# Attention over channels with a gated convolution: v transposed by DMA in 16-bit halves instead of on TensorE

## The chip, the cores and the metric

The kernel runs on one core of one Trainium2 chip. The metric is device time in microseconds (us) of one execution. Its engines are TensorE (PE; PEld is its weight load), VectorE (DVE), ScalarE (ACT), GpSimd (POOL) and SyncE (SP), which issues most DMAs. Before the change it takes 657.74 us, the median of two runs (656.74 and 658.73).

## The reference

q, k and v have shape (4, 6336, 256) in fp32. Attention is over the 256 channels, not over the 6336 rows; its result goes through a causal convolution with a sigmoid gate.

```python
def _attn_ref(q, k, v, tau):
    qn = q / (np.linalg.norm(q, axis=1, keepdims=True) + 1e-06)
    kn = k / (np.linalg.norm(k, axis=1, keepdims=True) + 1e-06)
    s = kn.transpose(0, 2, 1) @ qn / tau
    s = s - s.max(-1, keepdims=True)
    a = np.exp(s)
    a /= a.sum(-1, keepdims=True) + 1e-09
    return v @ a
...
    for k in range(K):          # K = 5
        gate_pre += conv_w[k][None, None, :] * xp[:, k:k + S, :]
    gate = 1.0 / (1.0 + np.exp(-gate_pre))
    val = x @ w_val
    return gate * val @ w_out
```

Here x is the attention's result and xp is x with four rows of zeros ahead.

## The kernel before, in words

Two kinds of work run side by side, for four batches each.

**Scores** (`score_group`). The rows of q and k come in 17 groups of three blocks per batch. For each group ScalarE casts the block to a reduced fp32 form, `hi` (L192), GpSimd subtracts to get the rest (L193), ScalarE squares (L209), VectorE and GpSimd add up the squares for the norms (L214: `acc_ps` on VectorE, `acc` on GpSimd), and TensorE multiplies hi and lo halves into `s_ps` (L226). After 17 groups `softmax(b)` makes the weights of batch b, plain ones for the gate and ones multiplied with w_val for the value.

**Steps of v**. Each batch of v has 13 chunks, twelve of 508 rows and one of 240, in all 52 steps. With four rows of overlap a chunk is 512 columns wide once it is transposed. For each step:

- `load_v` (L310) loads the chunk, rows on partitions, by DMA from SP's queue (L317 to L323). For the first chunk of a batch GpSimd clears four rows (L316).
- `transpose_v` (L328) has TensorE turn it in blocks of 128x128 into `t_ps` (L335), once for each half of the channels. ScalarE casts the result to `v_hi` (L336) and VectorE subtracts to get `v_lo` (L337).
- `conv` multiplies with the weights into `x_ps` (L345); ScalarE takes the first tap (L359) and VectorE the other four (L361), for each half.
- `sigmoid` on ScalarE (L367), `value` on TensorE into `val_ps` (L345) with VectorE's product (L374), `split_g` with a cast on ScalarE (L387) and a subtraction on GpSimd (`g_lo`, L388).
- `finish` multiplies with w_out into `o_ps` (L404), ScalarE copies it out (L414) and its queue stores it (L419, L421).

Groups of the next batches run between the steps of the current one: the loop at L532 spreads the groups that are left over the first 36 steps, so the last steps have no scores beside them. `VLEAD = 2` has a chunk turned two steps ahead of its use; `v_p` holds three chunks of `v_hi` and `v_lo`. The order that a reader sees in the code is a wish: a scheduler places the instructions on each engine, and each engine, and each DMA queue, works through its own list in order. An instruction that waits holds up everything behind it on its engine.

Of the kernel before, what the change touches and what calls it, by code (L numbers as in the profile page):

```python
# [28 lines left out]
def kernel(  # L29
# [280 lines left out]
    def load_v(b, i):  # L310

        t0, w = chunks[i]
        t = raw_p.tile([P, NT, C], F32, name="v_raw", bufs=3)
        j0 = 0
        if i == 0:
            nc.gpsimd.memset(t[0:HALO, 0, :], 0.0)  # L316
            nc.sync.dma_start(out=t[HALO:P, 0, :], in_=v[b, 0:P - HALO])  # L317
            j0 = 1
        full, rest = divmod(HALO + w, P)
        lo = t0 - HALO  # L320
        nc.sync.dma_start(out=t[:, j0:full, :], in_=v[b, lo + j0 * P:lo + full * P].rearrange("(j p) c -> p j c", p=P))
        if rest:
            nc.sync.dma_start(out=t[0:rest, full, :], in_=v[b, lo + full * P:t0 + w])  # L323
        vraw[b, i] = t

    def transpose_v(b, i, h):
        w = HALO + chunks[i][1]
        if h == 0:  # L328
            vt[b, i] = [v_p.tile([P, NH, HALO + WMAX], F32R, name=name) for name in ("v_hi", "v_lo")]
        th, tl = vt[b, i]  # L330
        src = vraw[b, i]
        tp = ps.tile([P, 512], F32, name="t_ps", tag="bank")
        for j in range(-(-w // P)):
            np_ = min(P, w - j * P)
            nc.tensor.transpose(tp[:, j * P:j * P + np_], src[0:np_, j, h * P:(h + 1) * P], ident[0:np_, 0:np_])  # L335
        nc.scalar.copy(th[:, h, 0:w], tp[:, 0:w])  # L336
        nc.vector.tensor_tensor(tl[:, h, 0:w], tp[:, 0:w], th[:, h, 0:w].bitcast(F32), ALU.subtract)  # L337
# [269 lines left out]
```

## Time and profile before

| | |
|---|---|
| runs | 656.74 and 658.73 us, median 657.74 |
| profiled execution, first to last instruction (span) | 653.8 us |
| TensorE busy | 636.1 us, 97% |
| VectorE busy | 521.7 us, 80% |
| ScalarE busy | 465.7 us, 71% |
| GpSimd busy | 362.1 us, 55% |
| TensorE's granted clock | 0.999 of full |
| moved by DMA | 105.75 MB, mean 162 GB/s |

The profile is of one execution. The page gives no time of that execution beside its span; the runs' median is 3.9 us longer. A group row reads: line, engine, operation, out<-in with shapes, count, then busy time in us and mean ns of one, then the engine's idle time just before them and what ended it. Lines are those of the kernel before. Matmuls are pipelined, so that the durations of single ones overlap; the chain of waits shows what they take in sequence.

### The profile page before, as it was taken

To read this page: it belongs to the slowest core of one execution; us is meant where nothing else is said; L and a number is where in the kernel's file an instruction comes from. 1 tells how busy PE (TensorE), PEld (TensorE's weight loads), DVE (VectorE), ACT (ScalarE), POOL (GpSimd) and SP (SyncE) were. 2 spreads that over 40 slices of the span, in tenths; PEclk is the share of its full clock that TensorE was granted. 3 is DMA by queue.
4 is the path that set the end of the run, shared out by engine and by line. 5 is a ranking of instruction groups with operands and counts; after the bars stand their busy time and mean duration, and the time that the engine had idled before them with its cause. 6 is when DMAs were issued, how large, how long until landed. Compare 5 with 4: busy or idle time off the path is not lost.

```text
span 653.8 us, 10657 instructions
## 1 busy us (share of the span) xinstructions
PE 636.1 (97%) x4008; PEld 570.3 (87%) x4008; DVE 521.7 (80%) x831; ACT 465.7 (71%) x607; POOL 362.1 (55%) x174
## 2 busy tenths in 40 slices
PE   7999999999999999999998999999999999999996
PEld 5878799998979999999997998999999798988886
DVE  3897689787878688778788688778778889888894
ACT  5465978867888768668688787777777755655564
POOL 2441896965837769659565497766763122312221
PEclk9999999999999999999999999999999999999999
DMA  8999875555635665545554375653222343443213
GB/s 272 336 320 335 267 233 154 152 170 162 188 99 175 186 195 176 167 136 173 177 178 127 113 222 168 179 182 103 65 80 76 113 126 102 114 129 105 65 51 99
DMA packets 107875, 105.75 MB, mean 162 GB/s; under 512 B 5744, under 2 KB 107312, under 8 KB 107824
## 3 DMA queue, kind: packets, MB, share of 16 engines
q1 hardware_dynamic: 82048, 79.76, 39.8%
q10 hardware_dynamic: 25776, 25.32, 13.7%
q8 instruction: 31, 0.51, 0.3%
q14 instruction: 20, 0.16, 0.1%
HBM read 79.11 MB, written 25.95 MB: 161 GB/s over the span
## 4 chain that ended last, share of the span: by engine, by line
PE 84%; DVE 4%; ACT 4%; DMA 3%; SPq 2%; POOL 1%; issue 1%; ACTq 0%; DVEq 0%
PE o_ps L404 21%; PE x_ps L345 19%; PE val_ps L345 19%; PE s_ps L226 17%; PE t_ps L335 6%; SPq L74 2%; DMA raw<-in_k_dram 1%; PE o_ps L294 1%; POOL hi L193 1%; DMA w_raw<-in_moe_conv_w_dram 1%; DMA v_raw<-in_v_dram 1%; ACT hi L192 1%; DVE acc_ps L214 1%; DVE gate L361 1%; DVE gate L374 1%
## 5 line engine op out<-in xcount | busy, mean ns | idle before, releaser
L361 DVE SCALAR_TENSOR_TENSOR gate<-x_ps,wa,gate 128x508 f32<-128x508 f32 (+1 forms) x416 | 275.4, 718 | 14.4 <-ACT gate L359 13.4
L193 POOL TENSOR_TENSOR hi<-raw,hi 128x1536 fp32r<-128x1536 f32 (+2 forms) x54 | 167.8, 3109 | 92.8 <-ACT hi L192 92.8
L388 POOL TENSOR_TENSOR g_lo<-gate,g_hi 128x1016 fp32r<-128x1016 f32 (+1 forms) x50 | 116.8, 2335 | 145.1 <-ACT g_hi L387 130.5
L214 DVE TENSOR_TENSOR acc_ps<-acc_ps,sq 128x512 f32<-128x512 f32 (+1 forms) x134 | 93.5, 698 | 73.9 <-ACT sq L209 70.7
L345 PE MATMUL x_ps<-v_hi,w 128*128 128x512 f32 (+1 forms) x416 | 138.1, 391 | 0.0
L345 PE MATMUL val_ps<-v_hi,w 128*128 128x508 f32 (+1 forms) x416 | 133.9, 384 | 0.8 <-ACT o_sb L414 0.7
L226 PE MATMUL s_ps<-hi 128*128 128x256 f32 (+1 forms) x852 | 121.0, 287 | 6.2 <-ACT hi L192 4.0
L226 PEld LDWEIGHTS s_ps<-hi 128*128 128x128 f32 (+1 forms) x852 | 110.7, 190 | 12.6 <-ACT hi L192 5.5
L404 PE MATMUL o_ps<-wo_hi,g_hi 128*128 128x256 f32 x400 | 113.3, 283 | 0.2 <-DVE gate L374 0.2
L414 ACT COPY o_sb<-o_ps 128x512 f32<-128x512 f32 x99 | 58.1, 588 | 76.1 <-PE o_ps L404 74.8
L404 PE MATMUL o_ps<-wo_lo,g_hi 128*128 128x256 f32 x400 | 112.2, 281 | 0.0
L404 PE MATMUL o_ps<-wo_hi,g_lo 128*128 128x256 f32 x400 | 111.8, 280 | 0.0
L209 ACT ACTIVATE sq<-raw 128x1536 f32<-128x1536 f32 (+3 forms) x69 | 96.0, 1393 | 16.3 <-DVE acc_ps L214 8.0
L214 POOL TENSOR_TENSOR acc<-acc,sq 128x512 f32<-128x512 f32 x58 | 76.3, 1315 | 38.9 <-ACT sq L209 38.5
L345 PEld LDWEIGHTS val_ps<-v_hi,w 128*128 128x128 f32 x416 | 77.2, 188 | 14.4 <-ACT o_sb L414 0.9
L345 PEld LDWEIGHTS x_ps<-v_hi,w 128*128 128x128 f32 x416 | 77.5, 188 | 13.9 <-DVE gate L361 0.2
L359 ACT ACTIVATE gate<-x_ps,wa 128x508 f32<-128x508 f32 (+1 forms) x104 | 68.1, 669 | 20.6 <-PE x_ps L345 20.3
L336 ACT CAST v_hi<-t_ps 128x512 fp32r<-128x512 f32 (+1 forms) x104 | 55.7, 568 | 35.7 <-PE t_ps L335 33.2
L345 PE MATMUL x_ps<-v_lo,w 128*128 128x512 f32 (+1 forms) x208 | 79.8, 384 | 0.0
L345 PE MATMUL val_ps<-v_lo,w 128*128 128x508 f32 (+1 forms) x208 | 79.3, 381 | 0.0
L374 DVE TENSOR_TENSOR gate<-val_ps,gate 128x508 f32<-128x508 f32 (+1 forms) x104 | 64.3, 657 | 17.1 <-ACT gate L367 14.4
L404 PEld LDWEIGHTS o_ps<-wo_hi,g_hi 128*128 128x128 f32 x400 | 75.3, 188 | 1.4 <-DVE gate L374 0.4
(84 smaller groups left out, 800.0 us busy)
## 6 DMA issues: line engine op xcount, KB each, us to landing
raw<-in_q_dram SPq DMA_DIRECT2D x64, 384.0 KB
raw<-in_k_dram SPq DMA_DIRECT2D x64, 384.0 KB
v_raw<-in_v_dram SPq DMA_DIRECT2D x44, 512.0 KB
out_dram<-o_sb ACTq DMA_DIRECT2D x47, 384.0 KB
out_dram<-o_sb ACTq DMA_DIRECT2D x47, 124.0 KB
v_raw<-in_v_dram SPq DMA_DIRECT2D x4, 384.0 KB
raw<-in_q_dram SPq DMA_DIRECT2D x4, 128.0 KB
raw<-in_k_dram SPq DMA_DIRECT2D x4, 128.0 KB
```

The costliest lines, as they stand in the source:

```text
L193: nc.gpsimd.tensor_tensor(hi[r, js, :, 1, :], raw[r, js, :, :], hi[r, js, :, 0, :].bitcast(F32), ALU.subtract)
L209: nc.scalar.activation(sq[0:np_, ja:jb], raw[0:np_, ja:jb], AF.Square)
L214: eng.tensor_tensor(st[key][0:np_], st[key][0:np_], sq[0:np_, j], ALU.add)
L226: nc.tensor.matmul(st["s"][:, h, :], lhs, rhs, start=False, stop=stop and h == NH - 1 and n_ == len(ops) - 1)
L336: nc.scalar.copy(th[:, h, 0:w], tp[:, 0:w])
L345: marks["PRODUCT"] = nc.tensor.matmul(ps, wt[:, which, ws, ch, hs], vs[:, ch, lo:hi_], start=n_ == 0, stop=n_ == 3 * NH - 1)
L359: nc.scalar.activation(gate[:, h, 0:w], x_ps[:, 0:w], AF.Copy, scale=cw[:, h, 0:1])
L361: nc.vector.scalar_tensor_tensor(gate[:, h, 0:w], x_ps[:, tap:tap + w], cw[:, h, tap:tap + 1], gate[:, h, 0:w], ALU.mult, ALU.add)
L374: nc.vector.tensor_tensor(gate[:, h, 0:w], val_ps[:, 0:w], gate[:, h, 0:w], ALU.mult)
L388: nc.gpsimd.tensor_tensor(gl[:, :, 0:w], gate[:, :, 0:w], gh[:, :, 0:w].bitcast(F32), ALU.subtract)
L404: nc.tensor.matmul(o_ps[:, u * C:(u + 1) * C], gs[:, h, off:off + P], ws[:, h, :], start=n_ == 0, stop=n_ == 3 * NH - 1)
L414: marks["ACT"] = nc.scalar.copy(o_sb[:, j:j + len(pair), :], o_ps[:, 0:len(pair) * C].rearrange("p (j c) -> p j c", c=C))
```

## The change

v no longer goes through TensorE. Each 32-bit word of v is seen as two 16-bit halves, so a row of 256 channels is 512 half words. One DMA a chunk now loads v and transposes it in the same go (`dma_start_transpose`, `load_v`): half word number c lands on partition c mod 128, in one of four columns of 512 rows, `v_cols`. The two halves of a channel are then on neighbouring partitions. Four DMAs (`spread_v`, L330 in the new numbering) move them: each takes every second partition of two columns, 64 partitions with two runs of 1 KB, so that both halves of a channel come to lie on the channel's own partition in `v_parts`. VectorE interleaves them into whole words, `v_word`, with two copies of 16-bit elements that write every second half word (`join_v`, L345). ScalarE casts `v_word` to `v_hi` in one go (L346), and GpSimd, not VectorE, subtracts to get `v_lo` (L347). GpSimd's clearing of four rows is gone; VectorE clears four columns for the first chunk of a batch (L342). Loads start one step earlier than before. New pool: three buffers of `v_cols`, two of `v_parts`; `v_word` has two.

```diff
-    def transpose_v(b, i, h):
-        w = HALO + chunks[i][1]
...
-        for j in range(-(-w // P)):
-            np_ = min(P, w - j * P)
-            nc.tensor.transpose(tp[:, j * P:j * P + np_], src[0:np_, j, h * P:(h + 1) * P], ident[0:np_, 0:np_])
-        nc.scalar.copy(th[:, h, 0:w], tp[:, 0:w])
-        nc.vector.tensor_tensor(tl[:, h, 0:w], tp[:, 0:w], th[:, h, 0:w].bitcast(F32), ALU.subtract)
+    vx_p = ctx.enter_context(tc.tile_pool(name="vx_p", bufs=3))
...
+        t = vx_p.tile([P, 2 * NH, SPAN], U16, name="v_cols")
+        nc.sync.dma_start_transpose(out=t[:, :, 0:rows], in_=v[b, lo:lo + rows].bitcast(U16))
...
+    def spread_v(b, i):
+
+        t, rows = vcols.pop((b, i))
+        d = vx_p.tile([P, 2, NH, SPAN], U16, name="v_parts", bufs=2)
+        half = P // 2
+        for x in range(2):
+            for s in range(2):
+                nc.sync.dma_start(out=d[x * half:(x + 1) * half, s, :, 0:rows],
+                                  in_=t[s:P:2, x:2 * NH:2, 0:rows])
+        vparts[b, i] = d, rows
...
+        vw = v_p.tile([P, NH, HALO + WMAX], F32, name="v_word", bufs=2)
...
+        halves = vw.bitcast(U16).rearrange("p h (t s) -> p h s t", s=2)
+        for h in range(NH):
+            nc.vector.tensor_copy(halves[:, h, :, c0:c0 + n], d[:, :, h, rows - n:rows] if i else d[:, :, h, 0:n])
+        nc.scalar.copy(th[:, :, 0:HALO + w], vw[:, :, 0:HALO + w])
+        nc.gpsimd.tensor_tensor(tl[:, :, 0:HALO + w], vw[:, :, 0:HALO + w], th[:, :, 0:HALO + w].bitcast(F32), ALU.subtract)
...
+    load_v(*step(VLEAD + 1))
+    spread_v(*step(1))
+    join_v(*step(0))
...
-        if step(n + VLEAD + 1):
-            load_v(*step(n + VLEAD + 1))
+        if step(n + VLEAD + 2):
+            load_v(*step(n + VLEAD + 2))
...
         if new:
-            for h in range(NH):
-                transpose_v(*new, h)
+            join_v(*new)
+        if step(n + VLEAD + 1):
+            spread_v(*step(n + VLEAD + 1))
```

The change shifts the code's lines: what was L193, L214, L361, L374 and L388 is now L195, L216, L371, L384 and L398. Three places show how the lists of the engines change.

GpSimd, amid steps that run beside scores, before (`hi` is the split of q and k, `acc` the sum of squares, `g_lo` the split of the gated value):

```order
L388 TENSOR_TENSOR g_lo<-gate,g_hi 128x1016
L193 TENSOR_TENSOR hi<-raw,hi 128x6x256
L214 TENSOR_TENSOR acc<-acc,sq 128x512
L388 TENSOR_TENSOR g_lo<-gate,g_hi 128x1016
L193 TENSOR_TENSOR hi<-raw,hi 128x6x256
L214 TENSOR_TENSOR acc<-acc,sq 128x512
```

And with the change:

```order
L398 TENSOR_TENSOR g_lo<-gate,g_hi 128x1016
L347 TENSOR_TENSOR v_lo<-v_word,v_hi 128x1024
L398 TENSOR_TENSOR g_lo<-gate,g_hi 128x1016
L195 TENSOR_TENSOR hi<-raw,hi 128x6x256
L216 TENSOR_TENSOR acc<-acc,sq 128x512
L347 TENSOR_TENSOR v_lo<-v_word,v_hi 128x1024
L195 TENSOR_TENSOR hi<-raw,hi 128x6x256
L216 TENSOR_TENSOR acc<-acc,sq 128x512
```

One `v_lo` of 1024 columns a step has come in among the others.

VectorE in the same part of the program, before (`gate<-x_ps` are the taps, `gate<-val_ps` the product with the value):

```order
L374 TENSOR_TENSOR gate<-val_ps,gate 128x508 x2
L337 TENSOR_TENSOR v_lo<-t_ps,v_hi 128x512 x2
L361 SCALAR_TENSOR_TENSOR gate<-x_ps,wa,gate 128x508 x8
L214 TENSOR_TENSOR acc_ps<-acc_ps,sq 128x512 x2
L374 TENSOR_TENSOR gate<-val_ps,gate 128x508 x2
```

And with the change:

```order
L384 TENSOR_TENSOR gate<-val_ps,gate 128x508 x2
L371 SCALAR_TENSOR_TENSOR gate<-x_ps,wa,gate 128x508 x3
L345 COPY v_word<-v_parts 128x2x512 x2
L371 SCALAR_TENSOR_TENSOR gate<-x_ps,wa,gate 128x508 x5
L216 TENSOR_TENSOR acc_ps<-acc_ps,sq 128x512 x4
L384 TENSOR_TENSOR gate<-val_ps,gate 128x508 x2
```

Two copies stand in place of the two `v_lo`, here between the third and the fourth of eight taps.

SP's queue, which issues the loads, before:

```order
L74 DMA raw<-in_q_dram 128x3x256
L74 DMA raw<-in_k_dram 128x3x256
L321 DMA v_raw<-in_v_dram 128x4x256
L74 DMA raw<-in_q_dram 128x3x256
L74 DMA raw<-in_k_dram 128x3x256
```

And with the change:

```order
L76 DMA raw<-in_q_dram 128x3x256
L76 DMA raw<-in_k_dram 128x3x256
L330 DMA v_parts<-v_cols 64x2x512 x4
L76 DMA raw<-in_q_dram 128x3x256
L76 DMA raw<-in_k_dram 128x3x256
L320 DMA_TRANSPOSE v_cols<-in_v_dram 128x4x512
L330 DMA v_parts<-v_cols 64x2x512 x4
```

Beside the loads of q and k there are now five DMAs for a chunk of v where there was one, and the moves read what an earlier transposition wrote.

More of the change, by code (lines that the diff above doesn't have):

```diff
@@ L11 @@
 I32 = mybir.dt.int32
+U16 = mybir.dt.uint16
 I64 = mybir.dt.int64
@@ L306 @@
     NT = -(-(HALO + WMAX) // P)
-    vraw, vt = {}, {}
+    SPAN = NT * P
+    vcols, vparts, vt = {}, {}, {}
     def load_v(b, i):
         t0, w = chunks[i]
[L313 to L324, printed above, removed]
@@ L326, in transpose_v @@
-    def transpose_v(b, i, h):
-        w = HALO + chunks[i][1]
[L328 to L332, printed above, removed]
-        for j in range(-(-w // P)):
-            np_ = min(P, w - j * P)
-            nc.tensor.transpose(tp[:, j * P:j * P + np_], src[0:np_, j, h * P:(h + 1) * P], ident[0:np_, 0:np_])
-        nc.scalar.copy(th[:, h, 0:w], tp[:, 0:w])
-        nc.vector.tensor_tensor(tl[:, h, 0:w], tp[:, 0:w], th[:, h, 0:w].bitcast(F32), ALU.subtract)
+        lo = max(t0 - HALO, 0)
@@ new lines, in load_v @@
+        rows = -(-(t0 + w - lo) // 16) * 16
+        lo = min(lo, N - rows)
+        t = vx_p.tile([P, 2 * NH, SPAN], U16, name="v_cols")
+        nc.sync.dma_start_transpose(out=t[:, :, 0:rows], in_=v[b, lo:lo + rows].bitcast(U16))
+        vcols[b, i] = t, rows
+    def spread_v(b, i):
[7 more added lines that the diff above has]
+        vparts[b, i] = d, rows
@@ new lines, in join_v @@
+    def join_v(b, i):
+        t0, w = chunks[i]
+        d, rows = vparts.pop((b, i))
+        vw = v_p.tile([P, NH, HALO + WMAX], F32, name="v_word", bufs=2)
+        th, tl = vt[b, i] = [v_p.tile([P, NH, HALO + WMAX], F32R, name=name) for name in ("v_hi", "v_lo")]
+        n = w + (HALO if i else 0)
+        c0 = HALO + w - n
+        if c0:
+            nc.vector.memset(vw[:, :, 0:c0], 0.0)
+        halves = vw.bitcast(U16).rearrange("p h (t s) -> p h s t", s=2)
[3 more added lines that the diff above has]
+        nc.gpsimd.tensor_tensor(tl[:, :, 0:HALO + w], vw[:, :, 0:HALO + w], th[:, :, 0:HALO + w].bitcast(F32), ALU.subtract)
@@ L504 @@
         run_group()
-        for h in range(NH):
-            transpose_v(*step(0), h)
+    spread_v(*step(0))
     tick()
@@ L520 @@
         tick()
-    for h in range(NH):
-        transpose_v(*step(1), h)
+    spread_v(*step(2))
+    join_v(*step(1))
     with behind("ACT"):
@@ L567 @@
         if new:
-            for h in range(NH):
-                transpose_v(*new, h)
+            join_v(*new)
+        if step(n + VLEAD + 1):
+            spread_v(*step(n + VLEAD + 1))
         tick()
```

## The prediction

> **What bounds the kernel now.** I read the page's table of busy time first, then the chain that ended last, then the busy time of each engine in stretches.
>
> ```profile
> span 653.8 us, 10657 instructions
> PE 636.1 (97%) x4008; PEld 570.3 (87%) x4008; DVE 521.7 (80%) x831; ACT 465.7 (71%) x607; POOL 362.1 (55%) x174
> PE 84%; DVE 4%; ACT 4%; DMA 3%; SPq 2%; POOL 1%; issue 1%; ACTq 0%; DVEq 0%
> ```
>
> TensorE (PE) has work 97% of the time and 84% of the chain lies on it. GpSimd (POOL) shows 55%, but an average over stages hides where that work lies. These stretches show it (columns: PE, weight loads, DVE, ACT, POOL in us; last the clock, the DMA share and GB/s).
>
> ```profile
> 60.00:491.00 431.00, 426.21 (x2793) 386.37 (x2792) 345.03 (x550) 334.66 (x422) 300.23 (x133) 1.00 0.55 165
> 491.00:654.00 163.00, 155.54 (x982) 138.98 (x980) 133.04 (x218) 97.44 (x152) 40.90 (x20) 0.99 0.34 98
> ```
>
> In the first stretch each step of v shares the engines with scores of the next batch; I call it the score stage. There GpSimd is busy 300 of 431 us, VectorE (DVE) 345. The second stretch is the tail, with steps of v alone. TensorE's share of the transposes shows in the chain, in order of time, over one step of the tail (start, duration, what):
>
> ```profile
> 580.62 2.73 PE val_ps L345 x12
> 583.36 0.87 PE t_ps L335 x8
> 584.23 2.74 PE x_ps L345 x12
> 586.97 2.83 PE o_ps L404 x24
> 589.80 2.73 PE val_ps L345 x12
> ```
>
> The step takes 9.18 us, all of it TensorE, and 0.87 us are the eight transposes of one chunk of v. (Their row in the groups has 273 ns each, but they are pipelined; 0.87 us for eight is the price on the path.)
>
> **The change, part by part.** *Removed on TensorE:* 400 transposes, 50 times eight, 50 x 0.87 = 43.5 us; 37 chunks or 32 us of it in the score stage, 13 chunks or 11 us in the tail. If nothing else stood in the way that is the gain.
>
> *Moved to GpSimd:* the lo half. The rows of the groups by form:
>
> ```profile
> L337 DVE TENSOR_TENSOR v_lo<-t_ps,v_hi 128x512 fp32r<-128x512 f32 x96 | 63.1, 682 | 11.0 <-ACT v_hi L336 11.0
> L336 ACT CAST v_hi<-t_ps 128x512 fp32r<-128x512 f32 (+1 forms) x104 | 55.7, 568 | 35.7 <-PE t_ps L335 33.2 <-DMA out_dram<-o_sb 2.6
> L388 POOL TENSOR_TENSOR g_lo<-gate,g_hi 128x1016 fp32r<-128x1016 f32 x47 | 113.1, 2405 | 140.3 <-ACT g_hi L387 125.7 <-DMA raw<-in_k_dram 9.5 <-issue 5.2
> L193 POOL TENSOR_TENSOR hi<-raw,hi 128x1536 fp32r<-128x1536 f32 x44 | 154.8, 3519 | 86.6 <-ACT hi L192 86.6
> L316 POOL MEMSET v_raw<- 4x256 f32 x4 | 1.2, 303 | 0.0
> ```
>
> What costs DVE 2 x 0.68 us costs GpSimd one subtraction of 128x1024, which by g_lo's row takes 2.4 us. ScalarE's two casts (2 x 0.57 us) become one over the same elements, no price. Every step has one operation more on GpSimd (its order is shown with the change); in the whole order 37 v_lo stand ahead of the last hi, the split of q and k. So GpSimd's work in the score stage is 300.2 + 37 x 2.405 - 3 x 0.3 = 388 us, of the 431 us it has now. Queued behind a late v_lo are the next hi, which TensorE's score products wait for, and g_lo, which the output products wait for.
>
> *Added on VectorE:* two copies of 16-bit words a chunk, 1024 elements each, SBUF to SBUF. No row shows a 16-bit copy. The nearest are the weights' steps, 512 words of 32 bits SBUF to SBUF, seen in the timelines of DVE and of POOL (start, duration):
>
> ```profile
> 26.01 1.49 DVE L132 TENSOR_SCALAR wb<-w_raw 128x512 int32<-128x512 int32 x1
> ...
> 31.09 0.43 DVE L136 TENSOR_SCALAR wb<-w_raw 128x512 int32<-128x512 int32 x1
> ...
> 36.81 1.23 DVE L144 TENSOR_SCALAR w_raw<-w_raw 128x512 int32<-128x512 int32 x1
> ```
>
> ```profile
> 25.64 1.58 POOL L214 TENSOR_TENSOR acc<-acc,sq 128x512 f32<-128x512 f32 x1 [3.19 <-ACT sq L209]
> ...
> 36.47 1.28 POOL L214 TENSOR_TENSOR acc<-acc,sq 128x512 f32<-128x512 f32 x1 [3.21 <-ACT sq L209]
> ```
>
> Alone such a step takes 0.43 us; 512 elements out of PSUM take 0.68 (v_lo's row), so it moves about two elements a cycle. With 1024 elements a copy is then about 0.68 us, 1.36 a chunk, just what the two v_lo took; at one element a cycle it would be 1.2. I take 0.68, since the copy too goes from SBUF to SBUF with one input.
>
> The same rows show the real price. L132 takes 1.49 us where its like takes 0.43: a GpSimd operation ran from 25.64 to 27.22, and the step ended 0.28 us later. L144 took 1.23 us: GpSimd was busy until 37.75, and it ended 0.29 us after. Such a step waits until GpSimd's operation is over, and those last up to 3.5 us (hi's row). In the score stage GpSimd is nearly always busy, so the copies wait, and while one finishes GpSimd stands. For 512 elements that was 0.28 us; for 1024, with 0.27 us more, 0.55 us.
>
> [...]
>
> In VectorE's new order the copies stand amid the taps of the convolution: when they wait, the taps behind them wait, and with them the sigmoid and g_hi.
>
> *Added DMAs:* one transposition in place of the load, and four moves of 64 partitions, all on SP's queue. Prices of today:
>
> ```profile
> DMA packets 107875, 105.75 MB, mean 162 GB/s; under 512 B 5744, under 2 KB 107312, under 8 KB 107824
> q1 hardware_dynamic: 82048, 79.76, 39.8%
> q10 hardware_dynamic: 25776, 25.32, 13.7%
> v_raw<-in_v_dram SPq DMA_DIRECT2D x44, 512.0 KB
> ```
>
> The queues hold 54% of 16 engines for 653.8 us, or 353 us; a packet of about 1 KB costs 353 x 16 / 107875 = 52 ns, a chunk's 512 packets 1.7 us. The moves are again 512 runs of 1 KB: 1.7 us a chunk, hidden at 55% DMA. The transposition is in no trace. Below: the load's 1.7 us. Above: each row falls into four destination groups of 256 bytes, 2048 pieces; at a full packet's 52 ns each, 6.7 us a chunk. I take the low end, since bytes and engines stay the same, and keep the high end for a rival. Hidden either way in one chunk; what may be late is the q and k loads, which stand behind moves and transpositions in SP's new order. The moves wait for the copies that free their target, two chunks back, and the transposition for moves. At 431 / 37 = 11.6 us a step that is hidden, unless the copies are late.
>
> [...]
>
> *Start:* the first chunk's path grows by moves, copies and a longer lo half. Today it is (chain):
>
> ```profile
> 49.27 5.56 DMA v_raw<-in_v_dram
> 60.91 0.87 PE t_ps L335 x8
> 69.99 2.76 PE x_ps L345 x12
> ```
>
> Landing at 55, first use at 70. The moves stand behind three more pairs of loads on SP; with some 5 us for moves, 1.4 for copies, 1.0 for the cast and 2.4 for lo they use up the slack. I put 0 to 10 us, take 3.
>
> **The sum**, against the span of 653.8 us. Score stage: GpSimd 388 + 74 copies x 0.55 = 429 us, as long as the stage is now, without a single idle moment. Today it idles 131 of 431 us, by its rows waiting for ScalarE; some of that stays. I take 5%: 429 / 0.95 = 452, so +21 us (0%: -2; 10%: +46). TensorE's need, 426 - 32 = 394, lies below; what it saves hides behind GpSimd. VectorE: 345 plus waits of about a half operation (1.2 us) for half to all of the copies, 390 to 434: near the same end. Tail: -11 if TensorE alone decides; VectorE's step there is read from this stretch of five steps:
>
> ```profile
> 560.00:606.00 46.00, 46.00 (x284) 40.96 (x283) 39.40 (x61) 27.03 (x41) 12.03 (x5) 1.00 0.37 109
> ```
>
> 39.4 of 46 us, or 7.9 us a step. It stays 7.9, since the copies take what the v_lo took, and gets one or two waits of some 0.6 us (half a GpSimd operation, and GpSimd busy half the time: 4.8 us a step): 8.5 to 9.1, against 8.31 left for TensorE and 9.18 now. I take -5 for the tail. Start +3. In all 653.8 + 21 - 5 + 3 = 672.8. The runs' median, 657.74, lies 3.9 over the span, so **676.7 us**, 2.9% slower.
>
> **The rivals.** (a) *Faster:* the copies don't meet the wait, because a 16-bit step moves in another way than the 32-bit ones or GpSimd's gaps take them. Then GpSimd needs 388 / 0.95 = 409: -22; tail -8; start +3: 653.8 - 27 + 3.9 = 631. For: 131 us of gaps now. Against: five sixths and more of the stage would be filled.
> (b) *No change:* GpSimd runs with almost no idle time, its waits for ScalarE being only slack of a stage paced by TensorE: -2 - 5 + 3, so 654, up to 668 at 3% idle.
> (c) *Much slower, DMA decides:* each 256-byte piece costs a packet. Score stage: 0.55 x 431 = 237 us, plus 37 x (6.7 - 1.7 + 1.7) = 248, 485 of 431; at 95% full 510, +79; start +7: about 743. It decides from 5.2 us a transposition on (431 - 237 = 194 over 37), or 41 ns a piece. Against: the same bytes over the same engines.
> [...]
> That the transposes stay on TensorE is excluded: its order has none of v.
>
> **How the numbers follow.** The forecast's mechanism, with 3 to 10% idle, 0.44; a quarter of that stays within 2% (idle under 4%); (a) 0.20; (b) 0.18; (c) 0.18. About 2% (13 us) can be told from no change. Faster 0.20; same 0.18 + 0.11, about 0.30; slower 0.50. The likeliest case alone spans 668 to 702. The range reaches to (a) and well towards (c): 632 to 725.
>
> **What would show it.** Right: no t_ps; v_lo on POOL near 2.4 us; the copies' mean far above their least duration, long ones ending about 0.55 us after a POOL operation; POOL above 85% of the score stage; gaps of TensorE before score products that wait for hi. Steps in the tail between 8.3 and 9.2 us. Wrong: copies all near 0.68 us, or near 1.2; TensorE still without gaps (a); DMA share above 90% with VectorE waiting for v_parts (c).

## The result and the profile after

The changed kernel takes **727.0 us** (median of 724.4 and 729.7) against 657.74: a ratio of 1.106 (95% interval 1.095 to 1.116). The forecast was 676.7, range 632 to 725: the direction was right, but the time lies above the range, and the loss was 69 us and not 19. The profiled execution has a span of 722.6 us; by spans the loss is 68.8 us.

The page of the changed kernel, its head, DMA lines and the chain that ended last:

```profile
span 722.6 us, 10232 instructions
PE 629.2 (87%) x3608; PEld 550.4 (76%) x3608; DVE 608.2 (84%) x835; ACT 467.2 (65%) x557; POOL 498.4 (69%) x222
DMA packets 215491, 132.03 MB, mean 183 GB/s; under 512 B 112272, under 2 KB 214928, under 8 KB 215440
q1 hardware_dynamic: 189664, 106.06, 66.0%
PE 35%; DVE 25%; DMA 12%; issue 9%; POOL 7%; ACT 7%; SPq 3%; ACTq 0%; DVEq 0%; POOLq 0%
```

Before, 84% of the chain lay on TensorE; now 35%, with 25% on VectorE. TensorE has 400 instructions less and is busy nearly as long, which the sum of its time explains: before 636.1 busy + 17.7 idle; now 629.2 busy + 93.4 idle. Without the transposes (43.5 us on the path) it should be busy 592.6, and a kernel below that has nothing in their place is at 593.1. So of the 68.8 us, 75.7 are new idle time, 36.6 are matmuls that became slower, less the 43.5 saved. The groups, of the changed kernel, show both: where TensorE waits, and that its matmuls are longer (417 ns, 391 before).

```profile
L355 PE MATMUL x_ps<-v_hi,w 128*128 128x512 f32 (+1 forms) x416 | 152.0, 417 | 48.7 <-DVE gate L371 42.3
L345 DVE COPY v_word<-v_parts 128x1024 uint16<-128x1024 uint16 (+2 forms) x104 | 152.7, 1516 | 15.5 <-DMA v_parts<-v_cols 10.7
L347 POOL TENSOR_TENSOR v_lo<-v_word,v_hi 128x1024 fp32r<-128x1024 f32 (+1 forms) x52 | 122.6, 2357 | 33.3 <-ACT v_hi L346 30.8
L216 POOL TENSOR_TENSOR acc<-acc,sq 128x512 f32<-128x512 f32 x58 | 84.7, 1460 | 37.8 <-ACT sq L211 37.5
L228 PE MATMUL s_ps<-hi 128*128 128x256 f32 (+1 forms) x852 | 122.5, 294 | 8.3 <-POOL hi L195 6.3
```

The copies have a mean of 1516 ns; their quickest for 1024 words take about 0.7. TensorE waits 42.3 us for `gate` on VectorE, the taps that must read `x_ps` before its buffer is free. The order of events in one place, first VectorE, then GpSimd, then TensorE's waits, of which the first is from the start of the program (start, duration, what, idle before):

```profile
280.65 0.75 DVE L371 SCALAR_TENSOR_TENSOR gate<-x_ps,wa,gate 128x508 f32<-128x508 f32 x1
281.31 4.59 DVE L345 COPY v_word<-v_parts 128x1024 uint16<-128x1024 uint16 x2
285.81 0.72 DVE L371 SCALAR_TENSOR_TENSOR gate<-x_ps,wa,gate 128x508 f32<-128x508 f32 x1
```

```profile
280.07 3.54 POOL L195 TENSOR_TENSOR hi<-raw,hi 128x1536 fp32r<-128x1536 f32 x1
283.55 1.75 POOL L216 TENSOR_TENSOR acc<-acc,sq 128x512 f32<-128x512 f32 x1
285.27 3.94 POOL L195 TENSOR_TENSOR hi<-raw,hi 128x1536 fp32r<-128x1536 f32 x1
```

```profile
93.78 1.21 PE L355 MATMUL val_ps<-v_hi,w 128*128 128x508 f32 x2 [6.34 <-ACT v_hi L346]
...
286.58 0.49 PE L355 MATMUL x_ps<-v_hi,w 128*128 128x512 f32 x1 [2.61 <-DVE gate L371]
```

Two copies that need 1.4 us took 4.59. They end 0.6 us after GpSimd's operations end (283.6 and 285.3): each waited until the operation that was running was over, and the next operation of GpSimd is longer by about 0.4 (1.75 for 1.31, 3.94 for 3.54). This is the rule and not one case: of the 88 copies of 1024 words 43 take over 1 us, and each of these 43 ends 0.60 to 0.63 us after an operation of GpSimd. The tap behind them comes at 285.81, and TensorE, idle for 2.61 us, goes on after that tap.

The slow matmuls follow such gaps. Stretches of the changed kernel near its start (PE, weight loads, DVE, ACT, POOL; last the granted clock, DMA share, GB/s):

```profile
93.00:99.00 6.00, 5.22 (x22) 5.05 (x23) 6.00 (x7) 3.47 (x3) 5.58 (x3) 0.50 1.00 275
105.00:111.00 6.00, 5.82 (x19) 4.62 (x19) 5.41 (x10) 4.25 (x5) 2.50 (x2) 0.72 1.15 248
123.00:129.00 6.00, 6.00 (x36) 5.27 (x35) 5.38 (x10) 5.43 (x6) 5.43 (x2) 1.00 1.26 190
```

After 6.34 us idle (until 93.78) the granted clock is 0.50 for the next six, and TensorE is busy 5.22 us with 22 matmuls, 20 of them on 256 columns; at full clock 36 fit into 6 us, half of them on about 510 columns. The mean over the execution is 0.947, before 0.999; over the span that is (0.999 - 0.947) x 722.6 = 37.6 us, close to the 36.6 above. The rows show this much: a clock of 0.50 behind the gap (93 to 99), 0.72 from 105 to 111, and 1.00 in a stretch without one (123 to 129, TensorE busy 6.00 of 6.00). What length of gap brings the clock down, and how soon it is back, they don't show.

Where along the program the time goes is read from the start of the last product of q and k, the row of `s_ps`, of the kernel before and of the changed one:

```profile
L226 PE MATMUL s_ps<-hi x852: 275/283/468, 38.5 to 497.9; 128*128 128x256 f32 x169, 64*128 64x256 f32 x2
```

```profile
L228 PE MATMUL s_ps<-hi x852: 274/283/580, 37.4 to 565.2; 128*128 128x256 f32 x169, 64*128 64x256 f32 x2
```

Up to there 67.3 us are lost, after it 1.5 (155.9 and 157.4 us to the end). For places between I use the start of `g_lo`, one a step, as lag behind the kernel before: 15 us at step 1, 40 at step 7, 36 at step 13, 61 at 25, 70 at 37, 69 at 51. (Neighbouring steps can differ by up to 11 us near the start.) So about 36 us are gone after thirteen steps, 34 more by the end of the scores, and the tail wins nothing.

### The profile page after: what moved, and what is told of

Read it like the earlier page. It is cut to its first block, busy times and chain, and to the rows that moved or that the text cites. A ratio compares the mean times of both kernels' runs of the same rounds, so it can differ in the third digit from the quotient of the medians.

```text
span 722.6 us, 10232 instructions
## 1 busy us (share of the span) xinstructions
PE 629.2 (87%) x3608; PEld 550.4 (76%) x3608; DVE 608.2 (84%) x835; ACT 467.2 (65%) x557; POOL 498.4 (69%) x222
## 4 chain that ended last, share of the span: by engine, by line
PE 35%; DVE 25%; DMA 12%; issue 9%; POOL 7%; ACT 7%; SPq 3%; ACTq 0%; DVEq 0%; POOLq 0%
PE x_ps L355 11%; PE o_ps L414 10%; DVE v_word L345 9%; DVE gate L371 9%; PE val_ps L355 8%; PE s_ps L228 5%; DMA v_parts<-v_cols 5%; DMA out_dram<-o_sb 4%; DVE acc_ps L216 4%; POOL hi L195 3%; DMA raw<-in_k_dram 2%; POOL v_lo L347 2%; ACT sq L211 2%; ACT hi L194 2%; POOL acc L216 1%
## 5 line engine op out<-in xcount | busy, mean ns | idle before, releaser
L371 DVE SCALAR_TENSOR_TENSOR gate<-x_ps,wa,gate 128x508 f32<-128x508 f32 (+1 forms) x416 | 282.7, 718 | 32.1 <-ACT gate L369 29.1
L398 POOL TENSOR_TENSOR g_lo<-gate,g_hi 128x1016 fp32r<-128x1016 f32 (+1 forms) x50 | 119.8, 2396 | 113.9 <-ACT g_hi L397 109.5
L355 PE MATMUL x_ps<-v_hi,w 128*128 128x512 f32 (+1 forms) x416 | 152.0, 417 | 48.7 <-DVE gate L371 42.3
L195 POOL TENSOR_TENSOR hi<-raw,hi 128x1536 fp32r<-128x1536 f32 (+2 forms) x54 | 173.5, 3216 | 22.2 <-ACT hi L194 20.7
L345 DVE COPY v_word<-v_parts 128x1024 uint16<-128x1024 uint16 (+2 forms) x104 | 152.7, 1516 | 15.5 <-DMA v_parts<-v_cols 10.7
L347 POOL TENSOR_TENSOR v_lo<-v_word,v_hi 128x1024 fp32r<-128x1024 f32 (+1 forms) x52 | 122.6, 2357 | 33.3 <-ACT v_hi L346 30.8
L355 PEld LDWEIGHTS x_ps<-v_hi,w 128*128 128x128 f32 x416 | 83.4, 202 | 69.3 <-issue 32.7
L216 DVE TENSOR_TENSOR acc_ps<-acc_ps,sq 128x512 f32<-128x512 f32 (+1 forms) x134 | 92.9, 693 | 25.9 <-ACT sq L211 22.3
L216 POOL TENSOR_TENSOR acc<-acc,sq 128x512 f32<-128x512 f32 x58 | 84.7, 1460 | 37.8 <-ACT sq L211 37.5
L369 ACT ACTIVATE gate<-x_ps,wa 128x508 f32<-128x508 f32 (+1 forms) x104 | 67.7, 666 | 42.3 <-PE x_ps L355 32.8
L377 ACT ACTIVATE gate<-gate 128x1016 f32<-128x1016 f32 (+1 forms) x52 | 52.9, 1018 | 58.2 <-DVE gate L371 57.6
L355 PE MATMUL x_ps<-v_lo,w 128*128 128x512 f32 (+1 forms) x208 | 85.4, 411 | 0.2 <-POOL v_lo L347 0.2
L384 DVE TENSOR_TENSOR gate<-val_ps,gate 128x508 f32<-128x508 f32 (+1 forms) x104 | 64.1, 656 | 23.3 <-ACT gate L377 21.0
L346 ACT CAST v_hi<-v_word 128x1024 fp32r<-128x1024 f32 (+1 forms) x52 | 52.7, 1013 | 47.9 <-PE val_ps L355 27.2
```

What stands on the lines that cost most here:

```text
L195: nc.gpsimd.tensor_tensor(hi[r, js, :, 1, :], raw[r, js, :, :], hi[r, js, :, 0, :].bitcast(F32), ALU.subtract)
L216: eng.tensor_tensor(st[key][0:np_], st[key][0:np_], sq[0:np_, j], ALU.add)
L345: nc.vector.tensor_copy(halves[:, h, :, c0:c0 + n], d[:, :, h, rows - n:rows] if i else d[:, :, h, 0:n])
L347: nc.gpsimd.tensor_tensor(tl[:, :, 0:HALO + w], vw[:, :, 0:HALO + w], th[:, :, 0:HALO + w].bitcast(F32), ALU.subtract)
L355: marks["PRODUCT"] = nc.tensor.matmul(ps, wt[:, which, ws, ch, hs], vs[:, ch, lo:hi_], start=n_ == 0, stop=n_ == 3 * NH - 1)
L369: nc.scalar.activation(gate[:, h, 0:w], x_ps[:, 0:w], AF.Copy, scale=cw[:, h, 0:1])
```

## The experiments

Theories. **P**: VectorE's copies wait for GpSimd's operations, and the taps behind them, and TensorE behind those, are late; GpSimd's added `v_lo` makes the waits more. **O**: it is enough that copies stand in an engine's order amid the operations that TensorE waits for. **A** and **C**: the DMAs (the moves, the transposition) are late. **G**: GpSimd's added work alone bounds the score stage. The first four expectations were written under other names, which they explain.

Every run is compared with the kernel before, timed beside it (657.1 to 658.2 us).

| run | us | ratio (95% interval) |
|---|---|---|
| e1_plain_load | 729.9 | 1.109 (1.105 to 1.112) |
| e2_act_copies | 727.7 | 1.107 (1.103 to 1.111) |
| e3_no_vlo | 702.3 | 1.067 (1.064 to 1.071) |
| e4_before_plus_transposes | 693.0 | 1.054 (1.050 to 1.057) |
| e5_no_moves | 710.6 | 1.082 (1.078 to 1.087) |
| e6_no_v_dma | 706.7 | 1.076 (1.072 to 1.079) |
| e7_start_on_pe | 717.1 | no interval; four executions of 705.1 to 721.3 us |
| e8_tail_dma | 681.6 | 1.036 (1.034 to 1.039) |
| e9_act_copies_dve_lo | 737.6 | 1.124 (1.121 to 1.127) |
| e10_no_dma_no_lo | 661.3 | 1.006 (1.003 to 1.008), without one execution of 1277 us |
| e11_no_dma_no_copies | 624.8 | 0.951 (0.950 to 0.953) |
| e12_no_dma_no_copies_no_lo | 617.8 | 0.941 (0.939 to 0.942) |
| e13_tail_dve_copies | 670.3 | 1.021 (1.016 to 1.026) |
| e14_tail_pool_copies | 669.5 | 1.019 (1.016 to 1.022) |
| e15_no_dma_act_copies | 681.1 | 1.036 (1.033 to 1.040) |
| e16_no_dma_idle_pool | 653.0 | 0.993 (0.991 to 0.995) |
| e17_idle_pool_no_copies | 632.5 | 0.962 (0.959 to 0.965) |
| e18_one_copy | 707.7 | 1.073 (1.066 to 1.081) |

### First: one suspect at a time

**e1_plain_load**, the transposition replaced by a plain load of the same bytes:

```diff
-        nc.sync.dma_start_transpose(out=t[:, :, 0:rows], in_=v[b, lo:lo + rows].bitcast(U16))
+        nc.sync.dma_start(out=t[:, :, 0:rows], in_=v[b, lo:lo + rows].bitcast(U16).rearrange("(p j) c -> p (j c)", p=P).rearrange("p (a r) -> p a r", r=rows))
...
-            nc.vector.tensor_copy(halves[:, h, :, c0:c0 + n], d[:, :, h, rows - n:rows] if i else d[:, :, h, 0:n])
+            nc.vector.tensor_scalar(halves[:, h, :, c0:c0 + n], d[:, :, h, rows - n:rows] if i else d[:, :, h, 0:n], 0xBFFF, None, ALU.bitwise_and)
```

> The transposing load is a plain load of the same bytes in 4 KB runs; moves, copies, cast and the lo half stay (the values are then not v transposed, and the copy masks one bit so that all words are finite). Theory 1, the loss lies in VectorE's copies waiting for GpSimd and in GpSimd's added work: 710 to 727 us, the copies' mean stays near 1.5 us. Theory 2, the transposition's own price on the DMA engines sets it: the DMA share of the first 150 us falls from over 1.0 to about 0.85, the 35 to 40 us that were lost by the seventh step go, 680 to 692 us. If both hold: 685 us with the copies' mean still above 1.3 us.

729.9 us, no gain. Nor is the start any better: the lag is 12 us at step 1, 41 at step 7, 45 at step 13. What the transposition costs more than a load is not what was lost.

**e2_act_copies**, the two copies on ScalarE:

```diff
-            nc.vector.tensor_copy(halves[:, h, :, c0:c0 + n], d[:, :, h, rows - n:rows] if i else d[:, :, h, 0:n])
+            nc.scalar.copy(halves[:, h, :, c0:c0 + n], d[:, :, h, rows - n:rows] if i else d[:, :, h, 0:n])
```

> The two interleaving copies go to ScalarE, all else stays. Theory 1: no VectorE instruction of a step needs what GpSimd holds, so the 82 us of waiting in the copies go and the 36 us that were lost between steps 13 and 34 with them: 680 to 695 us; ScalarE gets about 104 us more work and ends near 85 per cent. Theory 2: the start stays as it is, 715 to 730 us, with a DMA share of over 1.0 in the first 150 us. If both hold: about 690 us, with the first seven steps still 30 us late.

```profile
PE 628.5 (87%) x3608; PEld 550.3 (76%) x3608; DVE 468.8 (65%) x731; ACT 579.3 (80%) x660; POOL 477.2 (66%) x222
```

727.7 us, though VectorE's busy time falls from 608 to 469. ScalarE is at 80% and TensorE now waits for its `g_hi` (17.9 us) and for GpSimd's `hi` (17.1). By itself this speaks against P; e15 takes it up.

**e3_no_vlo**, `v_lo` left out, the products read zeros:

```diff
-        th, tl = vt[b, i] = [v_p.tile([P, NH, HALO + WMAX], F32R, name=name) for name in ("v_hi", "v_lo")]
+        th = v_p.tile([P, NH, HALO + WMAX], F32R, name="v_hi")
+        vt[b, i] = th, vzero
...
-        nc.gpsimd.tensor_tensor(tl[:, :, 0:HALO + w], vw[:, :, 0:HALO + w], th[:, :, 0:HALO + w].bitcast(F32), ALU.subtract)
```

> The lo half of v is left out: the products use a tile of zeros in its place, so GpSimd has 122 us less work; copies stay on VectorE. Theory 1: GpSimd is busy as before the change, the copies wait about half as long (mean about 1.1 us), 690 to 705 us. Theory 2: 715 to 727 us, the start unchanged.

702.3 us, 25 less. At step 13 it has lost as much as the changed kernel (36 us), at step 51 49 and not 69: `v_lo` costs in the score stage, not at the start.

**e4_before_plus_transposes**, the kernel before with a transposition of each chunk that nobody reads:

```diff
         vraw[b, i] = t
+        x = vx_p.tile([P, 2 * NH, NT * P], U16, name="v_cols")
+        nc.sync.dma_start_transpose(out=x[:, :, 0:rows], in_=v[b, lo:lo + rows].bitcast(U16))
```

> The kernel before with the transposing load added beside its own load of v, its result unused; no moves, no copies, TensorE transposes as before. The bytes through DMA are those of the changed kernel. Theory 1: the transposition is hidden, 657 to 665 us. Theory 2: the DMA engines are full in the first 150 us and q and k come late: 675 to 695 us.

693.0 us. The loss comes in the first 16 steps (37 us at step 16) and stays there (36 at step 51). The engines' work is that of the kernel before, so these 35 us come from the queues, where each chunk is now fetched twice. It made me look for the lost time in the DMAs, and that was the wrong place.

### Second: the DMAs taken out

**e5_no_moves** and **e6_no_v_dma**:

```diff
-        d = vx_p.tile([P, 2, NH, SPAN], U16, name="v_parts", bufs=2)
...
+        d = t.rearrange("p (s h) r -> p s h r", s=2)
```

In e5 `v_cols` has five buffers, as many as `v_cols` and `v_parts` had together. e6 leaves out the moves too, and here is what it leaves out besides:

```diff
-        t = vx_p.tile([P, 2 * NH, SPAN], U16, name="v_cols")
-        nc.sync.dma_start_transpose(out=t[:, :, 0:rows], in_=v[b, lo:lo + rows].bitcast(U16))
+        t = vfix
```

> The four moves of a chunk are left out: the copies read the transposed columns where they landed (with the same sizes and strides), the bytes that become v are not v's, and the copy is an AND with 0xBFFF so that every word stays finite. Every chunk keeps its transposition, its two copies on VectorE, its cast and its lo half on GpSimd. The changed kernel has lost 40 us at g_lo of step 7 and 69 us at the end. Theory A (the start is late because the moves stand behind pairs of raw loads on SP and land late, and because transposition, moves and copies wait for each other in turn): the lag at step 7 falls under 15 us and the time to about 700 us. Theory B (the lost time comes from the copies and the lo half on the engines, DMA is hidden): lag and time stay, 720 to 730 us. Theory C (the transposition's long issue on SP holds up the raw loads): the lag at step 7 stays above 20, since the transposition is still there; 705 to 725 us.

> No byte of v is loaded, transposed or moved: the copies of every chunk read one constant tile of zeros that is set once at the start, so the results are not v's. The engines' work is that of the changed kernel (two copies on VectorE with an AND, one cast, one lo half on GpSimd a chunk, no transposes on TensorE); the DMA engines have less than in the kernel before. Theory A or C (what is lost at the start is DMA): the lag of g_lo at step 7 is under 10 us, and what remains is the engines' loss: the kernel before plus about 25 us for the lo half (what leaving it out gave) minus some us in the tail, 670 to 690 us. Theory B (the engines alone lose it): lag 35 to 45 us at step 7 and 715 to 730 us.

710.6 and 706.7 us: the moves are worth 16 us, the transposition 4, and 49 of 69 us are lost with no DMA of v at all. Lags of `g_lo`:

| step | changed | e5, no moves | e6, no DMA | e11, no copies |
|---|---|---|---|---|
| 1 | 15 | 14 | 3 | 0 |
| 7 | 40 | 30 | 12 | -1 |
| 13 | 36 | 24 | 19 | -5 |
| 37 | 70 | 63 | 54 | -26 |
| 51 | 69 | 61 | 52 | -30 |

At step 13 36 us are lost: 12 by the moves, 5 by the transposition, 19 by the engines, and after it the DMAs add nothing. From step 13 to 37 the three kernels lose the same, 34, 39 and 35 us. A and C are right on a quarter of the loss, the engines on the rest. The page and the groups of e6:

```profile
PE 623.8 (88%) x3608; PEld 548.4 (78%) x3608; DVE 611.9 (87%) x836; ACT 468.6 (66%) x557; POOL 499.1 (71%) x222
L351 PE MATMUL x_ps<-v_hi,w 128*128 128x512 f32 (+1 forms) x416 | 147.1, 407 | 37.2 <-DVE gate L367 33.3
L341 DVE TENSOR_SCALAR v_word<-vfix 128x1024 uint16<-128x1024 uint16 (+2 forms) x104 | 155.0, 1539 | 4.0 <-POOL v_lo L343 3.9
```

The copies are as long as with DMAs, 1539 ns, and TensorE waits for the same taps.

**e7_start_on_pe**, chunks 0 to 7 on TensorE, from 8 on by DMA:

```diff
+    def by_dma(b, i):
+        n = b * NC + i
+        return n >= 8
...
     def join_v(b, i):
+        if not by_dma(b, i):
+            for h in range(NH):
+                transpose_v(b, i, h)
+            return
```

> The first eight chunks are loaded row by row and transposed on TensorE as in the kernel before, with their lo halves on VectorE; chunks 8 to 51 go the changed way. The computation is complete. Theory A or C (a start-up loss, by chunks that are needed before their DMAs can be there): lag of g_lo at step 7 at most 8 us, no new loss of 35 us when the changed way begins at step 8, and 727 - 30 to 40 = 685 to 697 us. Theory D (each change to the DMA way costs the same lead wherever it begins, because VectorE's waits and the queue lose it in the first steps after the change): the lag is small at step 7 and reaches 30 us within eight steps after step 8; 715 to 727 us.

717 us in the median, 705 in the fastest of four: not the 685 to 697 of A or C, but about the 715 to 727 of theory D, by which the way of DMA loses the same wherever it begins. The trace is of an execution of 718 us. The lag is 0 at step 4, 11 at 8, 17 at 13, 31 at 17 and 60 at 37: half of the start's loss is saved (17 us at step 13 for 36), and from there to step 37 another 44 us are lost (34 to 39 in the three kernels with copies of the table). A loss at the start of the program is not the main part.

### Third: copies and lo half, one without the other

All without DMAs of v. **e10** leaves `v_lo` out of e6 (as e3 does), **e11** the copies (the diff, against e6), **e12** both:

```diff
-        vw = v_p.tile([P, NH, HALO + WMAX], F32, name="v_word", bufs=2)
+        vw = vfix.rearrange("p a r -> p (a r)").bitcast(F32).rearrange("p (h r) -> p h r", h=NH)
...
-        for h in range(NH):
-            nc.vector.tensor_scalar(halves[:, h, :, c0:c0 + n], d[:, :, h, rows - n:rows] if i else d[:, :, h, 0:n], 0xBFFF, None, ALU.bitwise_and)
```

> As the run without any DMA of v (constant zeros as source, 706.7 us), and the lo half is left out too (the products read a tile of zeros in its place); two copies on VectorE and one cast a chunk remain, and GpSimd has no more than the kernel before. Theory P: the copies still wait behind GpSimd at 55%, mean about 1.2 us; leaving the lo half out gave 25 us in the run with DMAs: 675 to 690 us. Rival (with the DMAs gone the lo half is all that is left): 650 to 660 us.

> As the run without any DMA of v, and the two copies are left out too (the cast and the lo half read a constant tile of words); the lo half stays on GpSimd, so GpSimd's work is that of the changed kernel, 500 us, and VectorE's is 522 - 63 = 459. [...] Theory P (the waits of the copies, which hold up the taps behind them, are most of it): 640 to 660 us. Theory G (GpSimd's added 2.4 us a chunk itself is the bound of the score stage): 680 to 700 us, with TensorE waiting for hi of GpSimd.

> No DMA of v, no copies, no lo half: of the work on v only the cast of a constant tile is left, and TensorE has no transposes. This is what the removal of the transposes would bring with all that replaces them free: 658 - 43.5 = 614 us if TensorE alone sets it, and about 625 to 640 if ScalarE, VectorE and GpSimd already set part of the steps in the kernel before.

| | no lo half | lo half on GpSimd |
|---|---|---|
| no copies | 617.8 (e12) | 624.8 (e11) |
| two copies on VectorE | 661.3 (e10) | 706.7 (e6) |

The lo half alone costs 7 us, the copies alone 43.5, both 89: 38 us arise only from the two together. G is out. A stretch of the score stage of e11:

```profile
60.00:460.00 400.00, 392.03 (x2482) 354.00 (x2481) 305.70 (x473) 326.94 (x380) 370.45 (x163) 1.00 0.42 127
```

GpSimd works 370 of 400 us, 93%, and TensorE 392 at full clock: a GpSimd that is nearly full delays nobody as long as VectorE has no copy to wait for it.

### Fourth: is it the wait, or the place in the order?

**e16** leaves GpSimd without work (the lo halves of q, k, v and g and its sums of squares), with the copies of e6; **e17** is e16 without copies. **e15** is e6 with ScalarE's copies, edited as in e2. Of e16 the lines for q and k:

```diff
-            nc.gpsimd.tensor_tensor(hi[r, js, :, 1, :], raw[r, js, :, :], hi[r, js, :, 0, :].bitcast(F32), ALU.subtract)
...
-            eng, key = (nc.vector, "acc") if j < nv else (nc.gpsimd, "side")
+            if j >= nv:
+                continue
+            eng, key = nc.vector, "acc"
```

> No DMA of v, the copies on VectorE as in the changed kernel, and GpSimd left without work: the lo halves of q, k, v and g and GpSimd's sums of squares are left out, and the products read zeros in their place, so that TensorE, VectorE and ScalarE have the same instructions as in the run without DMA and without v's lo half (661.3 us). Theory P: every copy takes about 0.7 us, VectorE's busy time falls from 587 to about 535 us, and the time falls to 618 to 630 us, that of the runs without copies. Theory O: the copies cost their 43 us still, 650 us or more, less what TensorE no longer waits for GpSimd (6 to 12 us).

> As the run with GpSimd left empty (653.0 us, every copy 0.74 us), with the copies left out too: the cast reads a constant tile of words. Theory O (a copy costs TensorE its place amid the taps in VectorE's order, without any wait for GpSimd): about 615 us, that is 35 to 40 us below. Theory P (only the waits for GpSimd cost, and the other order that the program takes when GpSimd is empty accounts for the rest): 640 to 650 us.

> As the run without any DMA of v (706.7 us, zeros as source), but with the copies on ScalarE, so that VectorE has no operation that can wait for GpSimd: VectorE 469 us, ScalarE 580, GpSimd 500. Theory P (the waits for GpSimd are what the copies cost): near the run without copies, 624.8, and ScalarE's 80% a little over it: 630 to 650 us. Theory O (it is the copies' place in an engine's order, amid operations for which TensorE waits): 690 to 710 us, as on VectorE.

The copies' durations in e16 (least, median, most in ns), and in e10, where GpSimd has the work of the kernel before:

```profile
L345 DVE TENSOR_SCALAR v_word<-vfix x104: 431/744/768, 3.7 to 594.5; 128x1024 uint16<-128x1024 uint16 x88, 128x1016 uint16<-128x1016 uint16 x8, 128x488 uint16<-128x488 uint16 x8
```

```profile
L344 DVE TENSOR_SCALAR v_word<-vfix x104: 433/759/4147, 3.7 to 612.3; 128x1024 uint16<-128x1024 uint16 x88, 128x1016 uint16<-128x1016 uint16 x8, 128x488 uint16<-128x488 uint16 x8
```

With GpSimd empty no copy takes over 0.77 us: the waits are for GpSimd, as P has it. But e16 was not down at 618 to 630: the copies cost 653.0 - 632.5 = 20.5 us without any wait. So O seems to have its part: 1.4 us a step on VectorE, in order, ahead of taps. How large it is stays unsure. e17 has less to do than e12 and takes 632.5 - 617.8 = 14.7 us longer; nothing is added in it, but the scheduler chose another order of instructions, so order alone may be worth that much between two of these kernels. With GpSimd's old work the copies cost 43.5 us, with `v_lo` too 706.7 - 624.8 = 81.9. If the 20.5 may be carried over, a quarter of that 82 is place and three quarters are waits; the 82, the 43.5 and the 38 of the table are well above what order did, the 20.5 is not. On ScalarE no copy takes over 1437 ns (mean 1319), so none waits once begun, and they cost 681.1 - 624.8 = 56 us: less than on VectorE, more than nothing. They are 129.6 us in all, on an engine that is then at 85%. Both theories were too simple, P as well as O.

**e18_one_copy**, the changed kernel with one copy of 2048 words for two of 1024:

```diff
-        for h in range(NH):
-            nc.vector.tensor_copy(halves[:, h, :, c0:c0 + n], d[:, :, h, rows - n:rows] if i else d[:, :, h, 0:n])
+        part = d[:, :, :, rows - n:rows] if i else d[:, :, :, 0:n]
+        nc.vector.tensor_copy(halves[:, :, :, c0:c0 + n], part.rearrange("p s h t -> p h s t"))
```

> The computation is complete: the changed kernel, with one copy of 2048 words a chunk in place of two of 1024. If a copy waits once for a GpSimd operation whatever its size, 52 waits of about 0.8 us are gone from VectorE: its busy time falls from 608 to about 570 us, and the time to 705 to 715 us. Rival (the second copy of a pair mostly follows the first without a new wait, or a copy with one more dimension is slower): 720 to 735 us and VectorE at 600 us or more.

```profile
PE 625.5 (88%) x3608; PEld 550.3 (78%) x3608; DVE 573.4 (81%) x783; ACT 464.7 (66%) x555; POOL 501.0 (71%) x222
L345 DVE COPY v_word<-v_parts 128x2048 uint16<-128x2048 uint16 (+2 forms) x52 | 114.9, 2209 | 22.0 <-DMA v_parts<-v_cols 13.8
```

707.7 us, VectorE 573: as P said. The same words in half as many instructions save 38 us of copy time (152.7 to 114.9) and 19 us in all. A copy's mean is 0.80 us above its median of 1.41 now (2.21), and was 0.75 above a median of 0.76 (1.52): a wait is paid per instruction. It need not be a wait for one operation only: the longest copy of e18 takes 10.3 us and ends after the fourth operation of GpSimd that ran meanwhile.

### Fifth: versions that might beat both

**e9_act_copies_dve_lo**, copies on ScalarE and `v_lo` on VectorE:

```diff
-        nc.gpsimd.tensor_tensor(tl[:, :, 0:HALO + w], vw[:, :, 0:HALO + w], th[:, :, 0:HALO + w].bitcast(F32), ALU.subtract)
+        nc.vector.tensor_tensor(tl[:, :, 0:HALO + w], vw[:, :, 0:HALO + w], th[:, :, 0:HALO + w].bitcast(F32), ALU.subtract)
```

> The computation is complete: DMAs as in the changed kernel, the two copies of a chunk on ScalarE and the lo half on VectorE, so GpSimd does no more than in the kernel before and no copy on VectorE can wait for it. By the busy times of the runs so far: GpSimd 362 us, VectorE 469 + 52 x about 1.1 = 526, ScalarE 579. Theory P (VectorE's copies waiting behind GpSimd's operations, and GpSimd's added work, are what TensorE waits for; the DMAs add about 20 us): 665 to 685 us. Theory O (every chain of small operations in order costs it, whichever engine has them; ScalarE at 80% passes its lateness on as VectorE did): 700 to 725 us, with TensorE waiting for ScalarE's g_hi and o_sb.

```profile
L347 DVE TENSOR_TENSOR v_lo<-v_word,v_hi x52: 656/1620/4508, 76.5 to 703.1; 128x1024 fp32r<-128x1024 f32 x48, 128x488 fp32r<-128x488 f32 x4
```

737.6 us, worse than all. I had counted on 1.1 us for this subtraction and on no wait. For 1024 columns it takes 1.21 us at least and up to 4.5, and each of the longest 25 ends 1.08 or 1.09 us after an operation of GpSimd: here both inputs are in SBUF, and it waits for GpSimd as the copies do. In the kernel before one input was in PSUM, and there the 96 subtractions of 512 columns all take 0.68 to 0.69 us. ScalarE's copies in turn waited 43.8 us for this `v_lo` to free their buffer.

**e8**, **e13**, **e14**: only the 13 chunks of the tail by DMA, with the copies on ScalarE, VectorE, GpSimd (`by_dma` as in e7, the diff against e7):

```diff
-        return n >= 8
+        return n >= B * NC - NC
```

> Chunks 0 to 38 are transposed on TensorE as in the kernel before; only the 13 chunks of the last batch, used when the score work is over and GpSimd, ScalarE and the DMA queues have room, go the changed way, with their two copies on ScalarE. The computation is complete. If TensorE alone sets a step of the tail (0.87 us of transposes in 9.18): 13 x 0.87 = 11 us less than the kernel before, 647 us, down to 645. Rival (in the changed kernel the tail won only about 3 us, so that something else soon ends each step, VectorE or the waits between engines): 654 to 660 us, no difference that can be told.

> The computation is complete. As the run that had only the 13 chunks of the last batch by DMA, but with their copies on VectorE as in the changed kernel instead of on ScalarE. In the changed kernel the last 13 steps won 3 to 5 us over the kernel before. If that holds when only they are changed, and the loss of the run with ScalarE's copies (+24 us) came from ScalarE's order: 652 to 657 us. Rival (the DMA way costs its 20 to 25 us at each place where it begins, by its first chunks): 675 to 685 us.

> The computation is complete. Only the last 13 chunks by DMA, their copies on GpSimd, which also has their lo half: GpSimd is busy 41 of 163 us in the tail of the kernel before, VectorE then has 1.36 us a step less and no operation that waits for GpSimd. If TensorE sets the step then: 8.31 for 9.18 us, 647 us. Rival (GpSimd's four operations a step, 2.4 + 2.4 and two copies of 1 to 2.4 us, fill its step, 7 to 9.6 us, and the lo half of g comes late): 655 to 670 us.

681.6, 670.3 and 669.5 us, all slower than before. In e13 the lag is 3 us up to step 35, 20 at step 43 and 14 at 51: the first chunks of the new way come late, as rows of VectorE show, and the last eight steps win 6 us.

```profile
501.88 1.37 DVE L387 COPY v_word<-v_parts 128x1016 uint16<-128x1016 uint16 x2 [2.46 <-DMA v_parts<-v_cols]
513.27 1.36 DVE L387 COPY v_word<-v_parts 128x1024 uint16<-128x1024 uint16 x2 [3.85 <-DMA v_parts<-v_cols]
```

And there was little to win: in e12, with everything in place of the transposes free, the tail is 151.4 us for 155.9. Of the 11 us of transposes there only 4.5 lie on the path. No complete version was faster than the kernel before.

## Why the prediction was wrong, point by point

- *Transposes removed, 43.5 us.* Right as a price on TensorE: the span of e12 is 39.0 us shorter, 34.5 of them up to the last product of q and k (463.4 for 497.9) and 4.5 in the tail, where I had counted 11.
- *v_lo 2.4 us on GpSimd.* Right (2357 ns).
- *Copies 0.68 us alone, and waiting for GpSimd's operations.* Right: 0.74 with GpSimd empty, mean 1516 ns beside it. The rates behind it are estimates that the rows before bear out: v_lo takes 682 ns for 512 columns and 405 for 244, so 1.03 ns an element out of PSUM (the "cycle" of the estimate) and 0.15 us besides; with the same 0.15 us, the 0.43 us of 512 words in SBUF leave an estimated 0.54 ns a word, about half, and 512 more take 0.27 us. Where the estimate has 0.55 us behind GpSimd's operation, the long copies took 0.60 to 0.63.
- *The step that failed: "GpSimd 388 + 74 copies x 0.55 = 429", which made GpSimd the bound of the score stage, with VectorE "near the same end".* The wait was priced at the wrong engine, and the stage was taken to be as long as its fullest engine. No engine is full: in 445 us of the score stage VectorE is busy 392 (88%), TensorE 386 (87%) and GpSimd 362 (81% and not over 85), and 93% on GpSimd would do no harm (e11). What sets the pace is VectorE's list: copies of mean 1.5 us, behind them the taps, behind these `x_ps` on TensorE (42.3 us for `gate`, 6.3 for `hi`, which I had named as the sign). The copies lengthen GpSimd's operations by 498.4 - 477.2 = 21 us in all (changed kernel against e2, where VectorE has no copies), where 74 x 0.55 = 41 stood in the sum; with 21 the same sum gives (388 + 21) / 0.95 = 431 us, what the stage took before. That it came out as a loss at all was in this part luck. The score stage after step 13 lost 34 us where my +21 stood for the whole, and the copies' own place in the order, worth 20 us between e16 and e17 (as far as that can be trusted), was costed at nothing, since they take as long as the two `v_lo` did; that these stood better in VectorE's list is only argued. The score stage of the changed kernel:

```profile
100.00:545.00 445.00, 386.06 (x2314) 342.64 (x2312) 392.04 (x513) 305.56 (x351) 361.73 (x150) 0.94 0.83 186
```

- *Start, +3.* At step 1 15 us are gone, 12 of them with the DMAs (3 are left in e6); at step 13 it is 36, 17 of them DMAs, 19 the engines. SP's queue of the changed kernel there (without the loads of q and k), and what VectorE waits for behind it:

```profile
50.52 8.24 SPq L320 DMA_TRANSPOSE v_cols<-in_v_dram  x2
...
63.01 2.68 SPq L330 DMA_DIRECT2D v_parts<-v_cols  x4
...
73.31 1.70 SPq L330 DMA_DIRECT2D v_parts<-v_cols  x2
75.05 6.84 SPq L320 DMA_TRANSPOSE v_cols<-in_v_dram  x1
81.94 3.90 SPq L330 DMA_DIRECT2D v_parts<-v_cols  x6
```

```profile
86.31 6.33 DVE L345 COPY v_word<-v_parts 128x1024 uint16<-128x1024 uint16 x2 [5.24 <-DMA v_parts<-v_cols]
```

Transpositions hold SP for 2.4 to 6.8 us each here, moves stand behind them, the first chunk's are issued only at 63, and the second chunk's copies start at 86, 5.24 us after VectorE was free. I had counted what lands when, not how long SP's list takes. But that this long issue is what the start lost is not shown: in e1 a load of v holds SP for 0.35 us and the first moves are issued at 55, and the start is as late (12 us at step 1, 45 at step 13).
- *Tail, -5.* It lost 1.5. The waits of the copies were right, the gain was not there to be had.
- *The clock.* No term of mine: with gaps of TensorE the granted clock fell (0.50 behind the one of 6.34 us, mean 0.947 for 0.999), and the matmuls took 36.6 us more in all. Each us of new idle time came with about half a us of slower matmuls (36.6 for 75.7).
- *Rivals.* (c) needed 5.2 us of DMA for a transposition: e5 has 104065 packets more than e6 and (0.590 x 713.9 - 0.376 x 705.1) x 16 = 2497 us more of packet time, so 24 ns a piece and 3.1 us a chunk: between my bounds, nearer to the low one. DMA did not decide. (a) and (b) fell with the waits.

The direction came from the waits, which the rows of the weights' preparation had shown, and partly from luck; the size was lost by adding up busy time on one engine where a wait on another ran through three lists.

What stays open: which part of the queues costs the 17 us of the start (the lag at step 1 is 15 us, 14 without the moves, 12 with a plain load in place of the transposition); how much of e4's 35 us is the longer issue on SP and how much the added bytes; how much of the copies' cost is their place in the order; and why copies on ScalarE cost 56 us without DMAs and as much as VectorE's with them.

## What to carry to other kernels

An instruction that may have to wait for another engine is priced by what stands behind it in its own list, not by its busy time: make it one large instruction and not two (e18: 707.7 us for 727.0), and put it where nothing urgent follows (which no run here tried). Before work is moved off the engine that bounds the kernel, ask for the floor with the work simply left out, stage by stage; here it was 39 us, and every way to pay for it cost more. Gaps on TensorE cost more than their length here: 75.7 us of new idle time came with 36.6 us of slower matmuls, and behind a gap of 6.34 us the granted clock was 0.50.
